# Decay attention with two MLPs: two of three parts of queries and keys loaded as 104 and 24 rows, whole tokens rebuilt by VectorE behind the attention

## The chip, the cores and the metric

One core of one Trainium2 chip runs the whole program. The metric is device time in microseconds; before the change the median of three runs is 563.14 us (562.85 to 564.15). TensorE multiplies (its weight loads are shown as PEld), VectorE is DVE, ScalarE ACT, GpSimd POOL; SyncE (SP) issues most loads, which sixteen DMA engines carry.

## The reference

The inputs are q, k, v of shape (2, 8, 768, 64) and one decay per head. Tokens are taken in 12 chunks of 64:

```python
intra = np.einsum('bhic,bhjc->bhij', qb, kb) * Dmask[None]
intra = np.einsum('bhij,bhjd->bhid', intra, vb)
inter = np.einsum('bhid,bhde->bhie', qb * lam_pow[None], kv_state)
out[:, :, sl] = intra + inter
kv_state = lam_block * kv_state + np.einsum('bhsd,bhse->bhde', kb * rev_pow[None], vb)
```

The 1536 tokens of 512 values then go through two MLPs, 512 to 2048 to 512: the first with the gate `h * clip(h + 3, 0, 6) / 6`, the second with the gate `max(0.01 h, h)`. All in float32; the weights come as 64-bit words, of which the kernel makes float32 values by shifting and joining bits.

## The kernel before

**Attention.** For each chunk c of both batches: SP loads three parts of queries and keys (`load_qk`: part 0 queries, part 1 keys for the scores, part 2 keys in natural order) and, for two chunks at once, values (`load_v`). ScalarE copies the queries into PSUM (`queries`, tile `pair`), TensorE computes scores beside them (`s`), VectorE multiplies by the decay mask into `r` (`mask`), GpSimd scales the keys into `kd` (`k_decay`, two operations), TensorE makes the state (`t`, tile `a`) and the output (`o`, tile `h`), and ScalarE copies the state into the next chunk's values (`state_copy`, two). One copy of half of the values stands in another place of the tile `vs` (`part_v`): by ScalarE for chunks 0 to 2, by VectorE for 3 to 11. The output becomes tokens as a rounded part xh (ScalarE) and the rest xl (VectorE), `att_x`. For chunks 0 to 7 ScalarE also copies the output whole into `x_spare` (`att_spare`, line 362). Each of the pieces s, t, o is 32 matmuls in the trace.

**MLPs.** Weights are prepared by half slices (l, f, j): load (`raw`), two ScalarE activations, four VectorE operations, a ScalarE rounding (wh, line 457) and a VectorE difference (wl, line 461); `w0` holds four of a first matrix, `w1` five of a second. Slices f = 0 to 3 of the first MLP are multiplied directly, tile after tile (`gemm1`, `gemm2`). From f = 4 on, two token tiles and two slices form a two by two product with seven instead of eight products (`pair`): that takes sums of weights (S1 to S4; `w_sum`, `s_high`, `s_low`, tile `s`) and differences of tokens T1 to T4 (`sums_1`: `x_diff`, line 682, on the tokens in `x_spare`; then hi and lo parts by `x_split`, line 688 the lo). The spare tokens and the sums of weights share the two buffers `s`.

**Order.** `Order` is a list scheduler in Python: every operation has an engine, a guessed time, a due time (carried back from those who use it) and buffers that it takes and frees. It starts, of what is ready, the operation with the earliest due time as soon as its engine is free, and the engines' programs are written in that order. `DUE_C` are the attention's due times, `LATENCY` the time to another engine.

**Loads and borders.** TensorE's program comes in blocks of 256 instructions. `mm` counts them and notes the matmul 8 behind each border; `load` makes every six loads, from the sixteenth on, wait for the next border's matmul. `AT_BORDER` tells the list in which attention piece each border lies; `LOAD_ORDER` is SP's order of loads.

Lines: 148 all matmuls, 154 loads, 249 and 294 kd, 287 values, 312 queries, 320 mask, 334 state copies, 349 xl, 351 xh.

Of the kernel before, what the change touches and what calls it, by code (L numbers as in the profile page):

```python
# [36 lines left out]
T_FIRST, T_STEP, T_COLLECT, HOP = 40.0, 5.45, 2.0, 0.3  # L37
LATENCY = {"dma": 2.0, "pe": 0.15, "act": 0.15, "dve": 0.15, "pool": 0.15}
N_WARM, T_WARM = 9, 4.4
# [4 lines left out]
FIRST_LOADS, LOADS_PER_BLOCK = 15, 6  # L44
AT_BORDER = (('o', 0), ('s', 2), ('t', 3), ('s', 5), ('s', 6), ('s', 8), ('o', 8), ('s', 10))
LOAD_ORDER = (('qk', 0), ('v', 0), ('qk', 1), ('qk', 2), ('v', 2), ('qk', 3), ('qk', 4), ('v', 4), ('qk', 5), ('qk', 6), ('v', 6), ('qk', 7), (0, 0, 0), ('qk', 8), ('v', 8), ('qk', 9), ('qk', 10), ('v', 10), (0, 0, 1), ('qk', 11))
# [75 lines left out]
def decay_attention_two_mlps(ctx: ExitStack, tc: tile.TileContext, qkk, vv, lam, w1, w2, out):  # L122
    nc = tc.nc
    eng = {"act": nc.scalar, "dve": nc.vector, "pool": nc.gpsimd}

    sizes = {"raw": 3, "cv": 3, "cl": 2, "w0": 4, "w1": 5, "st": 2, "s": 2, "G": 3, "u": 3, "h": 2, "a": 2, "r": 3, "vs": 3}
    late = {"Gx": 3, "ux": 3}
    const = ctx.enter_context(tc.tile_pool(name="const", bufs=1))
# [23 lines left out]

    def load(out, in_):
        i = nc.sync.dma_start(out=out, in_=in_)  # L154
        k = (len(loads) - FIRST_LOADS) // LOADS_PER_BLOCK
        loads.append(i)
        if 0 <= k < len(AT_BORDER):
            tc.add_manual_dep(i.ins, borders[min(k, len(borders) - 1)].name, mybir.DependencyInfo(
                mybir.DependencyClass.Sync, mybir.DependencyReason.DATA), reason="behind the border")

# [98 lines left out]
    op_warm = add(("pe", T_WARM / 2), lambda _: dense(N_WARM - N_WARM // 2), -800, after=[op_lam])  # L259
    op_a = add(("dve", 1.5), consts_a, -100, takes=["u"] * 3 + ["r"])  # L260
    op_steps = add(("dve", 1.25), consts_b, -100, after=[op_lam, op_a], frees=["h"])
# [5 lines left out]
    def load_qk(c):  # L267
        def fn(_):
            for i in range(3):
                load(QK[c % NQ][:, i], qkk[c, :, i])  # L270
        return fn

    def load_v(c):

        def fn(_):
            vp = new("vs", [P, 2, 2, H, D], F32)
            VS[c], VS[c + 1] = vp[:, 0], vp[:, 1]
            for i in range(2):
                load(vp[:, i, 0], vv[c + i])
            if c == 0:  # L280
                nc.gpsimd.memset(vp[other[1], 0, 1], 0.0)
        return fn
# [70 lines left out]

    SPARE = {}

    def att_spare(c):
        def fn(_):
            j, i = divmod(c, SPT)
            if not i:
                SPARE[j] = pool["s"].tile([P, 2, 2, TT], F32, tag="s", name="x_spare")  # L360
            x = SPARE[j].rearrange("p j k (c b i) -> p (j k) c b i", c=SPT, b=2)[:, :, i]
            nc.scalar.copy(out=x, in_=PA["o", c])
        return fn

    x_ready, spared = {}, {}
    ld = {}
    for c in range(NSC):
        d = due_c[c] - 2.0
        ld["qk", c] = add(("dma", 2.05), load_qk(c), d, takes=["q"])
        ld["vp", c] = ld["vp", c - 1] if c % 2 else add(("dma", 1.4), load_v(c), d if c else 0.0, after=[ld["qk", c]], takes=["vs"])  # L370
        ld["v", c] = add(("act", 0.6 if c else 1.2) if c < 3 else ("dve", 0.5), part_v(c), d - 1.0, after=[ld["vp", c]])
    pieces = {}
    st, copies, masks, dense_ops, att_ops = {}, {-1: []}, [], [op_warm], []
    for c in range(NSC):
        d, last = due_c[c], c + 1 == NSC
        ks = [] if last else [add(("pool", 1.05), k_decay(c, b), d,
                                  after=[ld["qk", c], op_scan[b], st.get(c - 2)]) for b in ((1, 0) if c else (0, 1))]
        pe = ("pe", 1.15)
        qc = add(("act", 1.2) if c else ("none", 0.0), queries(c), d - 0.5, after=[ld["qk", c]], takes=["pair"])
        s = pieces["s", c] = add(pe, scores(c), d, after=[qc, op_warm])  # L380
        m = add(("dve", 1.13), mask(c), d + 1.2, after=[s, qc, op_const], takes=["r"] if c else [], frees=["pair"])
        masks.append(m)
        if c < 2:
            op_rows[1 - c] = add(("dve", 1.4), decay_rows(1 - c), d + 4.0, after=[m])
        add(("none", 0.0), nothing, after=[s, qc] + ks, frees=["q"])
        if not last:
            st[c] = pieces["t", c] = add(pe, state(c), d + 1.3, after=ks + [ld["v", c]] + copies[c - 1] + ([op_rows[c % 2]] if c else []),
                        takes=["a"])
            copies[c] = [add(("act", 0.58), state_copy(c, b), after=[st[c], ld["v", c + 1]]) for b in range(2)]
            add(("none", 0.0), nothing, after=copies[c], frees=["a"])  # L390
        o = pieces["o", c] = add(pe, attn_out(c), d + 2.6, after=[m, ld["v", c]] + copies[c - 1], takes=["h"])
        add(("none", 0.0), nothing, after=[o, st.get(c)], frees=["vs"] * (c % 2) + ["r"])
        for n, a in (("s", s), ("t", st.get(c)), ("o", o)):
            i = N_DENSE.get((n, c), 0)
            dense_ops += [add(("pe", 0.22 * i), lambda _, i=i: dense(i), d + 5.0, after=[a])] if i else []
        hi = add(("act", 0.58), att_x(c, False), d + 4.0, after=[o])
        x_ready[c] = add(("dve", 0.69), att_x(c, True), d + 5.0, after=[hi])
        if c < 2 * SPT:
            spared[c] = add(("act", 0.58), att_spare(c), d + 5.0, after=[hi], takes=["s"] * (not c % SPT))
        add(("none", 0.0), nothing, after=[x_ready[c], spared.get(c)], frees=["h"])  # L400
        att_ops += [x_ready[c], m, o, *ks, *copies.get(c, []), *([st[c]] if c in st else [])]
# [13 lines left out]
    def load_w(h):  # L415
        def fn(_):
            l, f, j = h
            RAW[h] = new("raw", [P, DM, 2], U32)
            raw, w = RAW[h].rearrange("p n t -> p (n t)"), (w1, w2)[l][f, j].bitcast(U32)
            for a in (slice(0, DM), slice(DM, 2 * DM)) if l + f < 2 else (slice(0, 2 * DM),):  # L420
                (load if h in LOAD_ORDER else nc.sync.dma_start)(raw[:, a], w[:, a])
        return fn
# [63 lines left out]

    composed, low = {}, {}
    for l in range(2):
        for f in range(NF):
# [11 lines left out]
            if paired(l, f) and f % 2:  # L501
                p, i = f // 2, None
                for n in range(4):
                    i = add(("dve", 0.43), w_sum(l, p, n), after=[composed[l, f - 1, 0], composed[l, f, 0], i])
                hi = add(("act", 1.05), s_high(l, p), after=[i], takes=["s"])
                s_ready[l, p] = add(("dve", 1.22), s_low(l, p), after=[hi], frees=["raw"])
                add(("none", 0.0), nothing, after=[i, low[l, f - 1, 0], low[l, f, 0]], frees=["cv"] * 2)
# [144 lines left out]

    XT, CS = {}, {}
    A_B = (("A11", "B11"), ("S1", "T1"), ("S2", "T2"), ("A12", "B21"), ("S3", "T3"), ("S4", "B22"), ("A22", "T4"))
# [22 lines left out]
    def spare(k, n):  # L677
        i = {"B11": 0, "T1": 0, "B21": 1, "T4": 1, "B12": 2, "T3": 2, "B22": 3, "T2": 3}[n]
        return SPARE[i // 2][:, i % 2]

# [3 lines left out]
    def x_split(k, n, lo, src):  # L684
        def fn(_):
            xh, xl = XT[k, n]
            if lo:
                nc.vector.tensor_tensor(out=xl, in0=src(k, n), in1=xh.bitcast(F32), op=ALU.subtract)
            else:
                nc.scalar.copy(out=xh, in_=src(k, n))  # L690
        return fn

# [280 lines left out]

    def sums_1():
        u = ("dve", 1.22)
        for n, t in (("B11", 0), ("B21", 0), ("B22", 1)):
            x_op[0, 0, n] = x_of(PAIR[t])
        t1 = add(u, x_diff(0, "T1", "B12", "B11", spare), after=list(spared.values()))
        t3 = add(u, x_diff(0, "T3", "B22", "B12", spare), after=[t1])
        t2 = add(u, x_diff(0, "T2", "B22", "T1", spare), after=[t3])  # L980
        t4 = add(u, x_diff(0, "T4", "B21", "T2", spare), after=[t2])
        for n, after in (("T1", [t2]), ("T2", [t4]), ("T4", [t4]), ("T3", [t3, last1[0, PAIR[1]]])):
            splits(0, 0, n, [op_late, *after], spare)
        done = [x_op[0, 0, n][0] for n in ("T1", "T4", "T3", "T2")]
        for d in (done[:2], done[2:]):
            add(("none", 0.0), nothing, after=d, frees=["s"])
# [72 lines left out]

    sums_1()  # L1060
    for b in range(SINGLE, len(BLOCKS[0])):
# [45 lines left out]
```

## Time and profile before

| | us |
|---|---|
| median of three runs | 563.14 |
| the profiled execution's own time | 563.63 |
| its span | 561.9 |
| TensorE busy | 548.5 |
| VectorE busy | 411.9 |
| ScalarE busy | 362.3 |
| GpSimd busy | 67.5 |

The span goes from the first to the last instruction. Busy times are sums over the instructions of an engine; one that waits is not busy. In a timeline row the bracket gives how long the engine had stood idle before the row and what ended that. "issue" there is time in which the engine waited for nothing that the profile shows. TensorE's granted clock is 1.0 in every stretch.

### The profile page before, as it was taken

To read this page: it belongs to the slowest core of one execution; us is meant where nothing else is said; L and a number is where in the kernel's file an instruction comes from. 1 tells how busy PE (TensorE), PEld (TensorE's weight loads), DVE (VectorE), ACT (ScalarE), POOL (GpSimd) and SP (SyncE) were. 2 spreads that over 40 slices of the span, in tenths; PEclk is the share of its full clock that TensorE was granted. 3 is DMA by queue.
4 is the path that set the end of the run, shared out by engine and by line. 5 is a ranking of instruction groups with operands and counts; after the bars stand their busy time and mean duration, and the time that the engine had idled before them with its cause. 6 is when DMAs were issued, how large, how long until landed. Compare 5 with 4: busy or idle time off the path is not lost.

```text
span 561.9 us, 9098 instructions
## 1 busy us (share of the span) xinstructions
PE 548.5 (98%) x3512; PEld 458.2 (82%) x3512; DVE 411.9 (73%) x690; ACT 362.3 (64%) x634; POOL 67.5 (12%) x77
## 2 busy tenths in 40 slices
PE   8888999999999999999999999999999999999996
PEld 5877888888788888888888888888888888888885
DVE  7879999987987974787689897686368943782342
ACT  5988895667666745578676886687268825683220
POOL 7651001101111101101000000000110110110000
PEclk9999999999999999999999999999999999999999
DMA  8984334534447433534200402241434622512332
GB/s 312 315 296 172 113 112 94 128 116 113 86 109 190 115 84 75 130 114 93 76 1 1 157 31 80 71 150 38 94 81 124 168 56 43 132 42 50 75 73 77
DMA packets 25596, 61.66 MB, mean 110 GB/s; under 512 B 3026, under 2 KB 3282, under 8 KB 25554
## 3 DMA queue, kind: packets, MB, share of 16 engines
q1 hardware_dynamic: 18672, 48.77, 26.8%
q0 software_dynamic: 6480, 11.80, 12.3%
q8 instruction: 27, 0.44, 0.4%
q10 hardware_dynamic: 402, 0.52, 0.3%
q14 instruction: 15, 0.12, 0.1%
HBM read 46.14 MB, written 3.15 MB: 88 GB/s over the span
## 4 chain that ended last, share of the span: by engine, by line
PE 90%; DVE 4%; DMA 2%; ACT 1%; issue 1%; POOL 1%; SPq 0%; DVEq 0%; POOLq 0%; ACTq 0%
PE acc L148 44%; PE h L148 27%; PE a L148 18%; DMA sums<-st 1%; DVE r L320 1%; DMA vs<-vv 1%; PE pair L148 1%; POOL kd L294 1%; DVE vs L287 1%; DVE t L441 0%; DVE u L550 0%; DVE t L451 0%; SPq L154 0%; DVE decay L242 0%; DVE Gl L563 0%
## 5 line engine op out<-in xcount | busy, mean ns | idle before, releaser
L580 POOL DMA_DIRECT2D sums<-st x45 | 39.5, 926 | 426.0 <-ACT st L636 426.0
L148 PE MATMUL acc<-Gl,wh 128*128 128x512 f32 x136 | 53.1, 390 | 0.1
L148 PE MATMUL acc<-Gh,wh 128*128 128x512 f32 x136 | 53.1, 390 | 0.0
L148 PE MATMUL acc<-Gh,wl 128*128 128x512 f32 x136 | 53.0, 390 | 0.0
L148 PE MATMUL acc<-wl,Gh 128*128 128x512 f32 (+1 forms) x128 | 49.6, 388 | 0.0
L148 PE MATMUL acc<-wh,Gh 128*128 128x512 f32 (+1 forms) x128 | 49.6, 387 | 0.0
L148 PE MATMUL acc<-wh,Gl 128*128 128x512 f32 (+1 forms) x128 | 49.5, 387 | 0.0
L451 DVE CUSTOM_DVE_ANT_0 t<-t,c 128x1024 uint16<-128x1024 uint16 x64 | 45.0, 704 | 2.2
L636 ACT COPY st<-acc 128x512 f32<-128x512 f32 x43 | 25.1, 587 | 32.1 <-PE acc L148 15.9
L428 ACT ACTIVATE c<-raw 128x512 uint32<-128x512 uint32 x64 | 42.7, 669 | 4.7 <-DVE t L451 3.1
L449 DVE SCALAR_TENSOR_TENSOR t<-raw,t 128x512 uint32<-128x512 uint32 x64 | 44.1, 688 | 1.1
L457 ACT CAST wh<-t 128x512 fp32r<-128x512 f32 (+1 forms) x64 | 37.7, 593 | 9.1 <-DVE t L451 6.2
L432 ACT ACTIVATE t<-raw 128x512 f32<-128x512 f32 x64 | 42.6, 667 | 0.0
L461 DVE TENSOR_TENSOR wl<-t,wh 128x512 fp32r<-128x512 f32 (+1 forms) x64 | 41.2, 652 | 0.7 <-ACT wh L457 0.4
L148 PE MATMUL a<-xh,wh 128*128 128x512 f32 (+1 forms) x108 | 38.9, 360 | 0.0
L566 DVE TENSOR_TENSOR Gl<-u,Gh 128x512 fp32r<-128x512 f32 x32 | 22.1, 689 | 22.9 <-ACT Gh L754 22.7
L148 PE MATMUL h<-xh,s 128*128 128x512 f32 x112 | 38.7, 390 | 0.0
L148 PE MATMUL a<-xh,wl 128*128 128x512 f32 (+1 forms) x108 | 38.7, 358 | 0.0
L148 PE MATMUL a<-xl,wh 128*128 128x512 f32 (+1 forms) x108 | 38.7, 358 | 0.0
L638 DVE TENSOR_TENSOR sums<-acc,sums 128x512 f32<-128x512 f32 x26 | 17.9, 690 | 28.0 <-PE acc L148 28.0
L438 DVE TENSOR_SCALAR t<-t 128x512 f32<-128x512 f32 x64 | 27.0, 422 | 15.3 <-ACT t L432 15.2
L760 ACT ACTIVATE u<-a 128x512 f32<-128x512 f32 x24 | 14.3, 597 | 25.8 <-PE a L148 25.8
(176 smaller groups left out, 1447.2 us busy)
## 6 DMA issues: line engine op xcount, KB each, us to landing
raw<-w SPq DMA_DIRECT2D x58, 512.0 KB, 3.3
sums<-st POOLq DMA_DIRECT2D x45, 256.0 KB, 4.1
sums<-qkk SPq DMA_DIRECT2D x36, 256.0 KB, 4.9
vs<-vv SPq DMA_DIRECT2D x12, 256.0 KB, 5.1
raw<-w SPq DMA_DIRECT2D x12, 256.0 KB, 4.1
out<-sums SPq DMA_DIRECT2D x19, 128.0 KB, 2.3
out<-sums ACTq DMA_DIRECT2D x3, 128.0 KB, 2.7
out<-sums SPq DMA_DIRECT2D x2, 64.0 KB, 2.3
```

The lines of the kernel that those rows point to most:

```text
L148: i = nc.tensor.matmul(out, a, x, **flags)
L428: nc.scalar.activation(out=CV[h][1], in_=RAW[h][:, :, 0], func=AF.Copy, scale=2.0 ** -29)
L432: return lambda _: nc.scalar.activation(out=CV[h][0].bitcast(F32), in_=RAW[h][:, :, 1].bitcast(F32), func=AF.Abs)
L438: nc.vector.tensor_scalar(out=t.bitcast(F32), in0=t.bitcast(F32), scalar1=MAG_MIN, scalar2=MAG_MAX, op0=ALU.max, op1=ALU.min)
L449: nc.vector.scalar_tensor_tensor(out=t, in0=RAW[h][:, :, 1], scalar=0xC0000000, in1=t, op0=ALU.bitwise_and, op1=ALU.bitwise_or)
L451: nc.vector.tensor_tensor(out=t, in0=t, in1=c, op=ALU.add)
L457: nc.scalar.copy(out=W[h][0][:, cols(*h)], in_=CV[h][0].bitcast(F32)[:, cols(*h)])
L461: return lambda e: eng[e].tensor_tensor(out=W[h][1][:, cols(*h)], in0=CV[h][0].bitcast(F32)[:, cols(*h)], in1=W[h][0].bitcast(F32)[:, cols ...
L566: nc.vector.tensor_tensor(out=gl, in0=U[s], in1=gh.bitcast(F32), op=ALU.subtract)
L580: return lambda _: nc.gpsimd.dma_start(out=SUM[t][:, e, :], in_=STAGE[t, e], accum_op=ALU.add)
L636: nc.scalar.copy(out=STAGE[t, e], in_=ps)
L638: nc.vector.tensor_tensor(out=acc, in0=ps, in1=acc, op=ALU.add)
```

## The change

Loads: from chunk 3 on, parts 1 and 2 of `load_qk` are two DMAs each, rows 0 to 103 and 104 to 127, and the parts come in the order 0, 2, 1. A load of two pieces counts once for the borders, and both pieces wait. `AT_BORDER` names other pieces.

Tokens: `att_spare` goes. `sums_1` rebuilds whole tokens as hi plus lo on VectorE (`x_whole`, four operations), after `op_late`, that is after all of the attention; the four differences come behind them. The tile `s` is opened with the late buffers, and the first sum of weights waits for the last whole token.

Values: the copies for odd chunks from 3 on are ScalarE's, those for even ones stay with VectorE.

List times: the load latency, masks, kd, values, and two set-up operations get other times.

```diff
-LATENCY = {"dma": 2.0, "pe": 0.15, "act": 0.15, "dve": 0.15, "pool": 0.15}
+LATENCY = {"dma": 2.5, "pe": 0.15, "act": 0.15, "dve": 0.15, "pool": 0.15}
-AT_BORDER = (('o', 0), ('s', 2), ('t', 3), ('s', 5), ('s', 6), ('s', 8), ('o', 8), ('s', 10))
+AT_BORDER = (('o', 0), ('o', 1), ('s', 4), ('t', 4), ('o', 5), ('s', 8), ('t', 8), ('o', 9))
+FEWER = (slice(0, 104), slice(104, 128))
+FEWER_FROM, FEWER_QK, FEWER_V, FEWER_RAW = 3, (1, 2), (), ()
...
-    sizes = {"raw": 3, "cv": 3, "cl": 2, "w0": 4, "w1": 5, "st": 2, "s": 2, "G": 3, "u": 3, "h": 2, "a": 2, "r": 3, "vs": 3}
-    late = {"Gx": 3, "ux": 3}
+    sizes = {"raw": 3, "cv": 3, "cl": 2, "w0": 4, "w1": 5, "st": 2, "G": 3, "u": 3, "h": 2, "a": 2, "r": 3, "vs": 3}
+    late = {"s": 2, "Gx": 3, "ux": 3}
...
-    def load(out, in_):
-        i = nc.sync.dma_start(out=out, in_=in_)
+    def load(out, in_, fewer=False):
         k = (len(loads) - FIRST_LOADS) // LOADS_PER_BLOCK
-        loads.append(i)
-        if 0 <= k < len(AT_BORDER):
-            tc.add_manual_dep(i.ins, borders[min(k, len(borders) - 1)].name, ...
+        loads.append(k)
+        for p in FEWER if fewer else (slice(0, P),):
+            i = nc.sync.dma_start(out=out[p], in_=in_[p])
+            if 0 <= k < len(AT_BORDER):
+                tc.add_manual_dep(i.ins, borders[min(k, len(borders) - 1)].name, ...
...
-    op_a = add(("dve", 1.5), consts_a, -100, takes=["u"] * 3 + ["r"])
+    op_a = add(("dve", 2.8), consts_a, -100, takes=["u"] * 3 + ["r"])
...
-            for i in range(3):
-                load(QK[c % NQ][:, i], qkk[c, :, i])
+            for i in (0, 2, 1):
+                load(QK[c % NQ][:, i], qkk[c, :, i], c >= FEWER_FROM and i in FEWER_QK)
...
-        ld["v", c] = add(("act", 0.6 if c else 1.2) if c < 3 else ("dve", 0.5), part_v(c), d - 1.0, after=[ld["vp", c]])
+        ld["v", c] = add(("act", 0.6 if c else 1.2) if c < 3 else ("act", 0.6) if c % 2 else ("dve", 0.8), part_v(c), d - 1.0, after=[ld["vp", c]])
...
-        ks = [] if last else [add(("pool", 1.05), k_decay(c, b), d,
+        ks = [] if last else [add(("pool", 1.15), k_decay(c, b), d,
-        m = add(("dve", 1.13), mask(c), d + 1.2, ...
+        m = add(("dve", 1.22 if c else 1.4), mask(c), d + 1.2, ...
-            op_rows[1 - c] = add(("dve", 1.4), decay_rows(1 - c), d + 4.0, after=[m])
+            op_rows[1 - c] = add(("dve", 2.1), decay_rows(1 - c), d + 4.0, after=[m])
...
-        x_ready[c] = add(("dve", 0.69), att_x(c, True), d + 5.0, after=[hi])
-        if c < 2 * SPT:
-            spared[c] = add(("act", 0.58), att_spare(c), d + 5.0, after=[hi], takes=["s"] * (not c % SPT))
-        add(("none", 0.0), nothing, after=[x_ready[c], spared.get(c)], frees=["h"])
+        x_ready[c] = add(("dve", 0.69), att_x(c, True), d + 5.0, after=[hi], frees=["h"])
...
+    def x_whole(k, n):
+        def fn(_):
+            if n == "B11" or n == "B22" and not k:
+                SPARE[k, int(n == "B22")] = pool["s"].tile([P, 2 << k, 2, TT >> k], F32, tag="s", name=f"x_spare{k}")
+            x = [part([x[i].bitcast(F32) for x in X], k, n) for i in range(2)]
+            nc.vector.tensor_tensor(out=spare(k, n), in0=x[0], in1=x[1], op=ALU.add)
+        return fn
...
-        t1 = add(u, x_diff(0, "T1", "B12", "B11", spare), after=list(spared.values()))
+        for n, t in (("B11", 0), ("B12", 1), ("B22", 1), ("B21", 0)):
+            w[n] = last_whole[0] = add(u, x_whole(k, n), after=[op_late, last_whole.get(0), *x_of(ts[t])],
+                                       takes=["s"] * (n == "B11" or n == "B22" and not k))
+        t1 = add(u, x_diff(k, "T1", "B12", "B11", spare), after=[w["B11"], w["B12"]])
+        t3 = add(u, x_diff(k, "T3", "B22", "B12", spare), after=[t1, w["B22"]])
+        t2 = add(u, x_diff(k, "T2", "B22", "T1", spare), after=[t3])
+        t4 = add(u, x_diff(k, "T4", "B21", "T2", spare), after=[t2, w["B21"]])
...
-    sums_1()
+    sums_1(0)
+    od.ops[s_at[0, starts[0][SINGLE] // 2]][3].append(last_whole[0])
```

## Rows read from the trace of the kernel before

**Rows 1.** The page, part 4: the chain that ended last, share of the span.

```profile
PE 90%; DVE 4%; DMA 2%; ACT 1%; issue 1%; POOL 1%; SPq 0%; DVEq 0%; POOLq 0%; ACTq 0%
```

**Rows 2.** Stretches: us; PE, PEld, DVE, ACT, POOL busy (count); PEclk, DMA share, GB/s.

```profile
10.00:46.00 36.00, 30.18 (x871) 27.57 (x868) 29.05 (x34) 31.11 (x56) 21.84 (x20) 1.00 0.93 318
46.00:60.00 14.00, 14.00 (x230) 11.71 (x225) 13.83 (x21) 12.68 (x23) 0.00 (x0) 1.00 0.27 91
60.00:78.00 18.00, 18.00 (x81) 14.87 (x81) 17.41 (x29) 16.51 (x32) 0.00 (x0) 1.00 0.40 128
78.00:108.00 30.00, 30.00 (x134) 24.86 (x133) 27.22 (x46) 20.77 (x35) 4.54 (x5) 1.00 0.45 116
...
160.00:560.00 400.00, 396.21 (x1908) 332.43 (x1906) 271.82 (x471) 240.41 (x425) 28.84 (x33) 1.00 0.33 86
```

**Rows 3.** Timeline, TensorE in the attention: start, us, engine, what, count, idle before.

```profile
14.40 1.15 PE L148 MATMUL h<-r,vs 128*64 128x64 f32 x32 [0.87 <-DVE r L320]
...
22.21 1.15 PE L148 MATMUL h<-r,vs 128*64 128x64 f32 x32 [0.78 <-DVE r L320]
...
25.75 1.15 PE L148 MATMUL pair<-sums 64*64 64x64 f32 x32 [0.24 <-ACT pair L312]
...
29.52 1.15 PE L148 MATMUL h<-r,vs 128*64 128x64 f32 x32 [0.60 <-DVE r L320]
...
31.84 1.97 PE L148 MATMUL pair<-sums 64*64 64x64 f32 x61 [0.91 <-issue]
...
44.54 0.30 PE L148 MATMUL a<-vs,kd 128*64 128x64 f32 x2 [1.23 <-POOL kd L294]
```

**Rows 4.** Timeline of the same stretch, ScalarE and VectorE.

```profile
11.89 0.59 ACT L362 COPY x_spare<-h 128x512 f32<-128x512 f32 x1
...
12.52 0.69 DVE L349 TENSOR_TENSOR xl<-h,xh 128x512 fp32r<-128x512 f32 x1 [1.41 <-ACT x_spare L362]
...
19.62 1.28 DVE L287 COPY vs<-vs 64x512 f32<-64x512 f32 x1
...
20.93 1.22 DVE L320 TENSOR_TENSOR r<-pair,decay 128x1024 f32<-128x1024 f32 x1
...
26.36 1.84 DVE L287 COPY vs<-vs 64x512 f32<-64x512 f32 x2
...
43.22 0.62 ACT L457 CAST wh<-t 128x512 fp32r<-128x512 f32 x1 [1.11 <-DVE t L451]
```

**Rows 5.** Groups by line and form, 0 to 62 us: busy, mean ns, idle before.

```profile
L362 ACT COPY x_spare<-h 128x512 f32<-128x512 f32 x8 | 4.7, 586 | 0.0
...
L287 DVE COPY vs<-vs 64x512 f32<-64x512 f32 x9 | 7.0, 799 | 0.2
...
L682 DVE TENSOR_TENSOR x_spare<-x_spare 128x1024 f32<-128x1024 f32 x2 | 2.4, 1220 | 0.0
```

**Rows 6.** Timeline: a wait for keys, its state product, two issues by SP.

```profile
22.10 2.18 POOL L294 TENSOR_TENSOR kd<-sums,decay 64x512 f32<-64x512 f32 x2 [1.49 <-DMA sums<-qkk]
...
27.82 1.10 PE L148 MATMUL a<-vs,kd 128*64 128x64 f32 x32
...
28.12 0.86 SPq L154 DMA_DIRECT2D vs<-vv  x2
```

**Rows 7.** Behind the attention: timeline of VectorE, weights and sums of weights.

```profile
71.27 0.69 DVE L461 TENSOR_TENSOR wl<-t,wh 128x512 fp32r<-128x512 f32 x1
...
76.95 1.31 DVE L461 TENSOR_TENSOR wl<-t,wh 128x512 fp32r<-128x512 f32 x2
...
100.16 1.22 DVE L484 TENSOR_TENSOR s<-raw,s 128x1024 fp32r<-128x1024 f32 x1
```

**Rows 8.** The chain in order of time, behind the attention: start, us, what, count.

```profile
72.47 2.72 PE h L148 x12
...
77.91 2.72 PE h L148 x12
...
111.91 2.72 PE h L148 x12
```

More of the change, by code (lines that the diff above doesn't have):

```diff
@@ L151, in mm @@
         records[0] += 4 if a.dtype == F32 else 2
-    def load(out, in_):
-        i = nc.sync.dma_start(out=out, in_=in_)
+    def load(out, in_, fewer=False):
         k = (len(loads) - FIRST_LOADS) // LOADS_PER_BLOCK
-        loads.append(i)
-        if 0 <= k < len(AT_BORDER):
-            tc.add_manual_dep(i.ins, borders[min(k, len(borders) - 1)].name, mybir.DependencyInfo(
-                mybir.DependencyClass.Sync, mybir.DependencyReason.DATA), reason="behind the border")
+        loads.append(k)
+        for p in FEWER if fewer else (slice(0, P),):
+            i = nc.sync.dma_start(out=out[p], in_=in_[p])
+            if 0 <= k < len(AT_BORDER):
+                tc.add_manual_dep(i.ins, borders[min(k, len(borders) - 1)].name, mybir.DependencyInfo(
+                    mybir.DependencyClass.Sync, mybir.DependencyReason.DATA), reason="behind the border")
     starts = [[sum(bs[:i]) for i in range(len(bs) + 1)] for bs in BLOCKS]
@@ L278, in fn @@
             for i in range(2):
-                load(vp[:, i, 0], vv[c + i])
+                load(vp[:, i, 0], vv[c + i], c >= FEWER_FROM and i in FEWER_V)
             if c == 0:
@@ L352, in att_x @@
         return fn
[L354 to L365, printed above, removed]
+    x_ready = {}
     ld = {}
@@ L380, in decay_attention_two_mlps @@
         s = pieces["s", c] = add(pe, scores(c), d, after=[qc, op_warm])
-        m = add(("dve", 1.13), mask(c), d + 1.2, after=[s, qc, op_const], takes=["r"] if c else [], frees=["pair"])
+        m = add(("dve", 1.22 if c else 1.4), mask(c), d + 1.2, after=[s, qc, op_const], takes=["r"] if c else [], frees=["pair"])
         masks.append(m)
         if c < 2:
-            op_rows[1 - c] = add(("dve", 1.4), decay_rows(1 - c), d + 4.0, after=[m])
+            op_rows[1 - c] = add(("dve", 2.1), decay_rows(1 - c), d + 4.0, after=[m])
         add(("none", 0.0), nothing, after=[s, qc] + ks, frees=["q"])
@@ L419, in fn @@
             raw, w = RAW[h].rearrange("p n t -> p (n t)"), (w1, w2)[l][f, j].bitcast(U32)
-            for a in (slice(0, DM), slice(DM, 2 * DM)) if l + f < 2 else (slice(0, 2 * DM),):
-                (load if h in LOAD_ORDER else nc.sync.dma_start)(raw[:, a], w[:, a])
+            for i, a in enumerate((slice(0, DM), slice(DM, 2 * DM)) if l + f < 2 else (slice(0, 2 * DM),)):
+                if h in LOAD_ORDER:
+                    load(raw[:, a], w[:, a], i in FEWER_RAW)
+                else:
+                    nc.sync.dma_start(out=raw[:, a], in_=w[:, a])
         return fn
@@ L485, in s_low @@
                                               in1=SB[l, p][:, 0].bitcast(F32), op=ALU.subtract)
-    composed, low = {}, {}
+    composed, low, s_at = {}, {}, {}
     for l in range(2):
@@ L504, in decay_attention_two_mlps @@
                     i = add(("dve", 0.43), w_sum(l, p, n), after=[composed[l, f - 1, 0], composed[l, f, 0], i])
-                hi = add(("act", 1.05), s_high(l, p), after=[i], takes=["s"])
+                hi = s_at[l, p] = add(("act", 1.05), s_high(l, p), after=[i], takes=["s"])
                 s_ready[l, p] = add(("dve", 1.22), s_low(l, p), after=[hi], frees=["raw"])
@@ L651, in store @@
         return fn
-    XT, CS = {}, {}
+    XT, CS, SPARE = {}, {}, {}
     A_B = (("A11", "B11"), ("S1", "T1"), ("S2", "T2"), ("A12", "B21"), ("S3", "T3"), ("S4", "B22"), ("A22", "T4"))
@@ L677, in spare @@
     def spare(k, n):
-        i = {"B11": 0, "T1": 0, "B21": 1, "T4": 1, "B12": 2, "T3": 2, "B22": 3, "T2": 3}[n]
-        return SPARE[i // 2][:, i % 2]
+        i = {"B11": 0, "T1": 0, "B12": 1, "T3": 1, "B22": 2, "T2": 2, "B21": 3, "T4": 3}[n]
+        return SPARE[k, 0][:, i] if k else SPARE[k, i // 2][:, i % 2]
     def x_diff(k, n, a, b, src):
@@ L972, in splits, with sums_1 @@
         x_op[l, k, n] = [add(("dve", 0.61 * u), x_split(k, n, True, src), after=[hi])]
-    def sums_1():
-        u = ("dve", 1.22)
+    last_whole = {}
+    def sums_1(k):
+        u, ts = ("dve", 0.61 * (2 - k)), (2, 2) if k else PAIR
         for n, t in (("B11", 0), ("B21", 0), ("B22", 1)):
-            x_op[0, 0, n] = x_of(PAIR[t])
-        t1 = add(u, x_diff(0, "T1", "B12", "B11", spare), after=list(spared.values()))
[L979 to L985, printed above, removed]
+            x_op[0, k, n] = x_of(ts[t])
+        w = {}
+        for n, t in (("B11", 0), ("B12", 1), ("B22", 1), ("B21", 0)):
[5 more added lines that the diff above has]
+        t4 = add(u, x_diff(k, "T4", "B21", "T2", spare), after=[t2, w["B21"]])
+        for n, after in (("T1", [t2]), ("T2", [t4]), ("T4", [t4]), ("T3", [t3, last1[0, ts[1]]])):
+            splits(0, k, n, after, spare)
+        done = [x_op[0, k, n][0] for n in ("T1", "T3", "T2", "T4")]
+        for d in (done,) if k else (done[:2], done[2:]):
             add(("none", 0.0), nothing, after=d, frees=["s"])
```

## The prediction

> **What bounds the kernel now.** I read the chain of waits first: nine tenths of it are TensorE's own matmuls [rows 1], so a change counts only where TensorE stands still. The table by stretches says where that is [rows 2]: from 46 us on TensorE is busy without a gap up to 108 us, and from 160 to 560 us it lacks 3.8 of 400 us; between 10 and 46 us, in the attention, it is busy 30.18 of 36, so 5.82 us stand idle. In the same stretch ScalarE is busy 31.11 us, VectorE 29.05, and the DMA engines have a share of 0.93. In the stretch from 46 to 78 us the roles are other: VectorE is busy 13.83 of 14 and 17.41 of 18 us, TensorE wholly.
>
> Then I went through TensorE's starts in the attention and took each with an idle time before it [rows 3]: 0.87, 0.78, 0.60, 0.91 and 1.23 us, and twice 0.24 (one row stands for both), 4.87 of the 5.82. The releasers differ: three waits for the mask (r, VectorE), two for the copied queries (pair, ScalarE), one in which nothing but TensorE's instruction supply ("issue") is late, and one put down to kd. Each has to be paid or removed by another part of the change.
>
> **Spare copies leave the attention.** Eight ScalarE copies of 0.586 us go, 4.7 us [rows 5]. One shows its harm: the copy at 11.89 us lies ahead of VectorE's subtraction, which waits 1.41 us in all and starts at 12.52, just as the copy ends [rows 4]; the next mask stands behind the subtraction on VectorE, and TensorE behind the mask (the 0.87). Without the copy the subtraction can start when the cast ahead of the copy ends, up to 0.59 us earlier; I count 0.5 of the 0.87, as the tail of a copy lies over its neighbour's start. The two waits of 0.24 for copied queries stand behind the same queue; I count both together at 0.3, as ScalarE is given new work.
>
> **Odd values to ScalarE.** VectorE's nine copies of values take 7.0 us, 0.80 each in the mean [rows 5]. The one at 19.62 takes 1.28, and the mask starts behind it at 20.93; two at 26.36 take 1.84 together, and they stand ahead of the next mask [rows 4]. Behind these masks TensorE waits 0.78 and 0.60 [rows 3]. Taking one of each pair away moves the mask by 0.9 (half of the pair) to 1.28 us, enough for both waits: 1.4 us. The price is five copies on ScalarE (chunks 3, 5, 7, 9, 11), 0.6 us each by the spare copy's row (512 elements as well, over twice the partitions), 3.0 us against the 4.7 saved. So ScalarE comes out 1.7 us ahead over all, less where both odd values and spare copies fall, which is why I gave its own two waits no more than 0.3. These copies wait for a load in ScalarE's order; queued behind them are the state copies, the queries and the casts, for which TensorE waits. If a load is late there, its whole lateness is TensorE's; that is in the first rival.
>
> **The stretch from 39 to 46 us.** The 1.23 us before 44.54 [rows 3] come while VectorE is the late engine: the two halves of the state copy, which that product needs, run on ScalarE behind a cast at 43.22 that waited 1.11 us for VectorE's weight work [rows 4]. That work has one odd value ahead of it, 0.80 in the mean, and it goes; I count 0.9 with the last of the spare copies, between nothing (the list puts something else there) and 1.23.
>
> **Loads in two pieces.** Chunks 3 to 11 get two more DMAs each, 18 in all. An issue costs SP 0.43 us (two in 0.86, [rows 6]), so 7.7 us of SP's time; the DMA engines carry the same bytes. The trace has no load of 104 or 24 rows. From below, the pieces may give back the wait for instructions, 0.91 us [rows 3], if its fetch finds less queued before it; from above, 12 of the 18 fall on chunks 3 to 8, while the DMA engines are nearly full, and 12 x 0.43 = 5.2 us of late landing is the most that the issues alone can do. Part 2, the natural keys, moves ahead of part 1; the row at 22.10 shows GpSimd waiting 1.49 us for such a load [rows 6], and the state product of that chunk starts at 27.82, 3.5 us after the two kd operations end at 24.28. So lateness up to some 3.5 us is covered there. I take a loss of 0.4 for both and no gain for the fetch: nearer to the covered side, as 6 loads of a border period need about 9 issues, 3.9 us, and four pieces of 1.15 us take 4.6.
>
> [...]
>
> **Whole tokens behind the attention.** Four sums of hi and lo are new on VectorE, and the four differences wait for them. All have the form of the difference, 128x1024 in 1.22 us [rows 5]: 4.9 us new, and the two differences that stood before 62 us move out of the attention's end, 2.4. So VectorE gets 7.3 us more between 60 us and the first use. The cover: VectorE idles 0.59 + 2.78 us from 60 to 108 [rows 2], and the sums of weights, last of that chain, start at 100.16, end 1.22 later, and are used from 111.91 [rows 7, 8], 10.5 us of lead. 3.4 + 10.5 = 13.9 > 7.3, so TensorE sees nothing at the first pair product, even when it comes 3 us earlier. It is nearer at the weights: wl at 71.27 ends at 71.96 for matmuls from 72.47 and the third of them uses it, and of the two at 76.95 the first ends at about 77.6 for 77.91 [rows 7, 8]. The lead is some 0.3 to 0.5 us (0.8 to 1.0 with the two matmuls before). TensorE can come earlier only as far as VectorE does. Before 78 us VectorE loses two differences (2.4), two odd values (0.9 to 2.0), and the other two differences (2.4) as long as no new sum is put in their holes: 3.3 to 6.8 us, more than the gain. I cost this at nothing.
>
> **List times and border names.** These change the order only. Where the list's time was too short (0.5 for a copy that takes up to 1.28), the new one fits the rows better. I give it nothing by itself, and 0.6 us either way in the range, the size of a difference of one operation in a queue.
>
> **Sum.** 0.5 + 0.3 + 1.4 + 0.9 - 0.4 = 2.7 us. The profiled execution took 563.63 us, its span 561.9 with 1.7 around it; it becomes 560.9. It lies 0.49 above the median of the three runs, 563.14, so the median becomes 560.4. What can be told from no change is 0.2%, 1.1 us.
>
> **Rivals.**
> (1) The loads come late and eat the gain. For it: the DMA share is 0.93 over the whole stretch, and GpSimd already waits 1.49 us for a load of keys [rows 2, 6]. Against it: the cover of 3.5 us. Half of the 5.2 us late, with TensorE 2.7 earlier, exceeds a cover of 3.5 by 1.8: 0.9 of the gain is left, 562.2; with all of the gain lost 563.1. [...]
> (2) Everything goes: the seven waits and the rest of the 5.82 us but the part of the first (0.37), with the fetch. 5.4 us, 557.7. Against it: ScalarE had 31.11 of 36 us of work and keeps about 30.
> (3) Slower: new sums are taken up early. The list starts whatever is ready when VectorE is free, and behind the attention eight operations of 1.22 us are ready at once. If six stand ahead of the weights of 72 and 78 us, 7.3 us, against 4.4 freed for certain to be elsewhere (two differences and two odd values at their longest), VectorE is 2.9 late, and with 0.9 of lead TensorE stands 2.0 us at 72 to 78, and the attention's gain is not passed on: 565.1. It decides from the third sum on: with two, 2.4 us, the freed time pays.
> (4) The fetch gets worse: six borders lie between 15 and 42 us, one costs 0.91 now. If four do, 2.7 more, the gain is gone: 563.1.
>
> **Chances.** Forecast 0.52, rival (2) 0.12, (1) 0.16, (3) 0.12, (4) 0.08. Faster by over 1.1 us holds the forecast, (2) and a little of (1), and loses a little of the forecast's low side: 0.64. Within: 0.20, from (1), (4) and that side. Slower: 0.16, (3) and the worse part of (1) and (4). The likeliest case alone has 558.8 to 561.8; the range reaches to rival (2) below and to the start of (3) above, 557.6 to 564.2.
>
> **What would show it.** TensorE's busy time between 10 and 46 us, or the idle time in it, falls from 5.82 to about 3; TensorE's two waits for r behind copies of values are gone; VectorE's copies of values are five fewer; no wait of TensorE between 46 and 110 us. The share and GB/s of the DMA engines in 10 to 30 us, and GpSimd's waits for keys, decide on the pieces; the idle time with releaser "issue" decides on the fetch. I am wrong if TensorE waits for wl between 60 and 80 us, if ScalarE waits for values, or if the idle time comes back as waits for loads.

## The result: slower by 0.9%

| | before | after |
|---|---|---|
| median of 6 runs (us) | 563.57 (562.85 to 564.77) | 568.83 (567.66 to 570.28) |
| profiled execution, its span | 563.63, 561.9 | 570.28, 568.5 |
| TensorE busy in the span | 548.5 | 550.0 |

The ratio is 1.0092 (1.0073 to 1.0111). The forecast was 560.4 us, at most 564.2: the change is slower where a gain was expected, and by more than any of the rivals allowed. The page's chain that ended last answers [rows 1]; its second line has the shares by line and tile.

```profile
PE 88%; DMA 7%; ACT 1%; DVE 1%; SPq 1%; issue 1%; POOL 1%; DVEq 0%; ACTq 0%; POOLq 0%
PE acc L150 45%; PE h L150 26%; PE a L150 17%; DMA sums<-qkk 4%; DMA raw<-w 2%; DMA sums<-st 1%; SPq L159 1%; POOL kd L297 1%; PE pair L150 0%; ACT u L538 0%; DVE decay L245 0%; ACT pair L315 0%; DVE a L736 0%; DVE u L542 0%; ACT st L628 0%
```

Transfers hold 7% of the span where they held 2%, and "sums<-qkk", the loads of queries and keys, 4% by themselves. The stretches (columns as in [rows 2]; 60 to 160 replaces the last two stretches there) say where:

```profile
10.00:46.00 36.00, 27.47 (x746) 25.26 (x742) 19.23 (x23) 26.09 (x46) 18.29 (x17) 0.95 0.94 251
30.00:40.00 10.00, 6.00 (x163) 5.39 (x165) 3.00 (x4) 6.37 (x12) 3.46 (x4) 0.99 0.99 242
40.00:50.00 10.00, 8.94 (x226) 8.30 (x223) 8.14 (x11) 7.99 (x14) 6.16 (x6) 0.84 0.87 242
46.00:60.00 14.00, 11.77 (x268) 10.31 (x268) 11.67 (x17) 11.07 (x20) 3.96 (x4) 1.00 0.87 253
60.00:160.00 100.00, 99.64 (x495) 82.14 (x492) 91.61 (x150) 72.68 (x125) 7.95 (x9) 1.00 0.37 98
```

TensorE stands idle 8.53 us of the first 36 (before 5.82), and 2.23 between 46 and 60, where it had no gap [rows 2]. The DMA engines are as full as before, 0.94, and move 251 GB/s instead of 318; the loads are therefore not done at 46 us, and the share stays at 0.87 up to 60, where it was 0.27. Between 40 and 50 us the granted clock is 0.84: it is 0.50 from 39.8 to 43.0 and 1.00 from 43.2 on, behind 10 us in which TensorE had been busy for 6.00; that the one brought the other is not shown. Two pieces show the clock, 1.97 and 1.74 us where such a piece takes 1.15 [rows 3]:

```profile
28.00 0.97 PE L150 MATMUL a<-vs,kd 128*64 128x64 f32 x26 [0.91 <-issue]
...
32.51 0.30 PE L150 MATMUL a<-vs,kd 128*64 128x64 f32 x2 [1.46 <-issue]
...
38.32 0.30 PE L150 MATMUL a<-vs,kd 128*64 128x64 f32 x2 [1.77 <-issue]
...
39.90 1.97 PE L150 MATMUL h<-r,vs 128*64 128x64 f32 x31
41.80 1.74 PE L150 MATMUL pair<-sums 64*64 64x64 f32 x32
```

The account against the kernel before: 2.71 us more idle in 10 to 46, 2.23 in 46 to 60, 0.25 in 60 to 160 (0.36 against 0.11), and 1.5 of TensorE's own time, nearly all of it the two pieces at the lower clock (0.82 + 0.59), 6.7 us together; the spans differ by 6.6. The medians differ by 5.3: the profiled execution is the slowest of the six.

Who waited for loads, 10 to 60 us (total, times, longest):

```profile
POOL kd L297 <- DMA sums<-qkk: 8.7, 5, 2.9
...
ACT vs L290 <- DMA vs<-vv: 5.0, 2, 3.3
```

GpSimd's waits for keys were 3.5 us before. VectorE waited 4.4 us for values. TensorE's waits in 10 to 62 us are 10.7 in all, most of them here:

```profile
PE a L150 <- issue: 4.1, 3, 1.8
PE h L150 <- DVE u L542: 1.6, 1, 1.6
PE pair L150 <- DMA sums<-qkk: 1.2, 2, 1.0
PE pair L150 <- ACT vs L337: 1.1, 2, 0.7
PE h L150 <- issue: 0.9, 1, 0.9
PE pair L150 <- issue: 0.7, 1, 0.7
```

"issue" has 5.7 us of them (before 1.1), but it is not all instruction supply. 2.5 us fall inside a piece, as before 28.00, where the next block of 256 instructions begins: such waits, before 15.96, 21.69 and 28.00, lie 125 and 126 matmuls apart, with their weight loads 250 and 252 of the 256 (before the change 0.91, at 31.84 [rows 3]). The other 3.2, before 32.51 and 38.32, stand at the first matmuls of two state products, and these start 0.1 us after the first of ScalarE's two state copies (0.58 each) has ended. The copies stood behind work of ScalarE that had waited for loads of values and of weights:

```profile
31.19 0.61 ACT L290 COPY vs<-vs 64x512 f32<-64x512 f32 x1 [3.35 <-DMA vs<-vv]
31.83 1.18 ACT L337 COPY vs<-a 64x512 f32<-64x512 f32 x2
...
36.95 0.66 ACT L420 ACTIVATE c<-raw 128x512 uint32<-128x512 uint32 x1 [2.23 <-DMA raw<-w]
37.64 1.18 ACT L337 COPY vs<-a 64x512 f32<-64x512 f32 x2
```

With the 0.5 before the second copies, 3.7 of the 10.7 us came this way; none is put down to kd, on whose keys GpSimd waited longest.

The DMA engines' own rows show the cause (15 to 40 us; the queue of the loads: packets, MB, share of 16 engines; the first fence is of before):

```profile
DMA packets 4107, 7.57 MB, mean 303 GB/s; under 512 B 452, under 2 KB 452, under 8 KB 4101
...
q1 hardware_dynamic: 4101, 7.47, 89.5%
```

```profile
DMA packets 3436, 6.15 MB, mean 246 GB/s; under 512 B 463, under 2 KB 463, under 8 KB 3432
...
q1 hardware_dynamic: 3432, 6.08, 94.5%
```

Share x 16 x 25 us, over the packets that are not small ones under 512 B, is the mean time of one 2 KB packet: 98 ns before, 127 after (over all packets 87 and 110; the expectations below give the middle one before, 84). The bytes are the same; each row takes 30% longer.

The other rows of the list [rows 5]: the eight spare copies are gone; ScalarE's values take 0.6 us each, as costed, but waited 5.0 us for loads from 10 us on; the four sums take 1.22 each, as costed.

### The profile page after: what moved, and what is told of

The parts are those of the page before. It is cut to its first block, busy times and chain, and to the rows that moved or that the text cites. A ratio compares the mean times of both kernels' runs of the same rounds, so it can differ in the third digit from the quotient of the medians.

```text
span 568.5 us, 9119 instructions
## 1 busy us (share of the span) xinstructions
PE 550.0 (97%) x3512; PEld 459.8 (81%) x3512; DVE 412.5 (73%) x689; ACT 361.0 (63%) x631; POOL 68.0 (12%) x77
## 4 chain that ended last, share of the span: by engine, by line
PE 88%; DMA 7%; ACT 1%; DVE 1%; SPq 1%; issue 1%; POOL 1%; DVEq 0%; ACTq 0%; POOLq 0%
PE acc L150 45%; PE h L150 26%; PE a L150 17%; DMA sums<-qkk 4%; DMA raw<-w 2%; DMA sums<-st 1%; SPq L159 1%; POOL kd L297 1%; PE pair L150 0%; ACT u L538 0%; DVE decay L245 0%; ACT pair L315 0%; DVE a L736 0%; DVE u L542 0%; ACT st L628 0%
## 5 line engine op out<-in xcount | busy, mean ns | idle before, releaser
L555 DVE SCALAR_TENSOR_TENSOR Gl<-u,Gh 128x512 fp32r<-128x512 f32 x36 | 24.6, 686 | 9.3 <-ACT Gh L548 9.2
```

Source lines behind the costliest of these rows:

```text
L555: nc.vector.scalar_tensor_tensor(out=gl, in0=U[s], scalar=1.0 / 6.0, in1=gh.bitcast(F32), op0=ALU.mult, op1=ALU.subtract)
```

## The experiments

Theory R, formed from these rows: the loads' pieces make every packet slower, and all that is lost is lost there; the rest of the change gains. Rivals: the second issue by SP is the cost (I); the order of the parts or the new border names are the cost (O); the values on ScalarE are.

**e1_whole_loads.** The changed kernel with whole loads.

```diff
-FEWER_FROM, FEWER_QK, FEWER_V, FEWER_RAW = 3, (1, 2), (), ()
+FEWER_FROM, FEWER_QK, FEWER_V, FEWER_RAW = 3, (), (), ()
```

> The changed kernel with every load whole again (128 rows), all else as changed. Theory A, the pieces of 104 and 24 rows slow every packet of the loads (2 KB packets between 15 and 40 us took 84 ns in the middle before the change and 105 to 133 after it): the loss goes and the rest of the change shows its gain, 561 us (559 to 562.5), with 320 GB/s or more between 10 and 30 us. Theory B, the 18 further DMAs cost (issues, completions): the same, 561 us. Theory C, the list order, the borders, the odd values or the whole tokens cost: 567 us or more, with the idle time of TensorE in the attention still near 11 us.

561.99 us against 563.29 of before, 0.9974 (0.9958 to 0.9990). Each set against the kernel before of its own job, the pieces cost 5.26 + 1.30 = 6.6 us, and the rest of the change gains 1.3. The packet is back at 0.931 x 400 / (4348 - 487) = 96 ns:

```profile
q1 hardware_dynamic: 4348, 7.91, 93.1%
```

TensorE's idle time in 10 to 46 us falls to 3.97, and it has no gap from 46 to 160:

```profile
10.00:46.00 36.00, 32.03 (x906) 29.32 (x901) 28.16 (x32) 31.57 (x55) 22.47 (x20) 1.00 0.97 331
46.00:60.00 14.00, 14.00 (x198) 11.74 (x198) 11.60 (x21) 13.10 (x23) 0.00 (x0) 1.00 0.26 91
60.00:160.00 100.00, 100.00 (x442) 82.53 (x441) 92.13 (x151) 71.39 (x121) 10.57 (x12) 1.00 0.41 106
```

**e2_split_alone.** The kernel before with the pieces alone.

```diff
-                load(QK[c % NQ][:, i], qkk[c, :, i])
+                load(QK[c % NQ][:, i], qkk[c, :, i], c >= 3 and i in (1, 2))
```

> The kernel before with nothing but the two pieces (parts 1 and 2 from chunk 3 on, in the old order 0, 1, 2, old borders). A and B: 568 to 571 us, as the old order has less slack than the changed one. C: 563.5 us, no change.

571.93 us, 1.0148 (1.0127 to 1.0170): 8.6 us lost by the pieces alone, with the old order of parts and the old borders. So neither the order (O) nor the values are the cause; what else is in the change even took some of the loss back. A packet took 0.938 x 400 / (3501 - 472) = 124 ns.

```profile
q1 hardware_dynamic: 3501, 6.21, 93.8%
```

**e3_halves_of_columns.** As many DMAs as in the changed kernel, cut by columns: 128 rows of 1 KB.

```diff
-FEWER = (slice(0, 104), slice(104, 128))
+FEWER = (slice(0, 4), slice(4, 8))
-            i = nc.sync.dma_start(out=out[p], in_=in_[p])
+            i = nc.sync.dma_start(out=out[:, p], in_=in_[:, p])
```

> The changed kernel with the same loads in two pieces, but cut by columns: 128 rows of 1 KB each, twice. As many DMAs as the changed kernel. A: the rows lie as in a whole load, so about 561.5 us, as with whole loads. B: as slow as the changed kernel, 568 us.

563.51 us, 1.0005 (0.9992 to 1.0018); 1.5 us above e1 of the same job. That is the most that the second DMA (I) can have cost, 1.5 of the 6.6, for these pieces also have twice the packets, of 1 KB; cutting by rows is the other 5.1. The stretch from 10 to 46 us keeps its rate:

```profile
10.00:46.00 36.00, 31.86 (x903) 29.16 (x899) 26.46 (x31) 31.28 (x55) 22.55 (x20) 1.00 0.96 309
```

**e4_loads_alone.** A program of loads alone, in phases of twelve loads of 256 KB (or of a part of their rows), each phase cut in another way.

```diff
+    rows = [whole, (slice(0, 104), slice(104, 128)), (slice(0, 64), slice(64, 128)), (slice(0, 112), slice(112, 128)),
+            (slice(0, 104),), (slice(0, 24),), None, whole]
```

> Only loads, nothing of the computation: twelve loads of 256 KB (or a part) after one another in eight phases: whole; 104 and 24 rows; 64 and 64; 112 and 16; 104 alone; 24 alone; two halves of columns; whole again. A: whole loads near 340 to 400 GB/s with packets of 84 ns; 104 and 24 rows at 240 to 270 GB/s with packets of 105 to 135 ns; halves of columns above 320. 64 and 64 rows slower still if it is a matter of which rows move together. B: halves of columns as slow as 104 and 24 rows, and packets of 104 and 24 rows still 84 ns.

Stretches inside the phases (clock, DMA share, GB/s at the end): whole, 104 and 24 rows, 64 and 64, halves of columns, whole; then SP's issues in the phase of 64 and 64.

```profile
1.00:11.50 10.50, 0.00 (x0) 0.00 (x0) 1.00 0.87 300
13.00:27.50 14.50, 0.00 (x0) 0.00 (x0) 1.00 0.74 217
28.50:45.80 17.30, 0.00 (x0) 0.00 (x0) 1.00 0.65 182
...
83.00:96.00 13.00, 0.00 (x0) 0.00 (x0) 1.00 0.82 242
98.00:108.00 10.00, 0.00 (x0) 0.00 (x0) 1.00 0.90 315
```

```profile
28.38 15.26 SPq L135 DMA_DIRECT2D x<-qkk  x24
```

The loss is there without any computation beside it: 217 GB/s in 104 and 24 rows (219 in 112 and 16) against 300 to 315. By the division above a packet took 95 ns whole and 111 in 104 and 24 rows, and the engines' share fell from 0.87 to 0.74: each is about half of the loss. The phase of 64 and 64 rows tells nothing of the DMA engines, though it is the slowest: SP needed 15.3 us for its 24 issues, 0.64 each where halves of columns took 0.47, and they fill the stretch. Halves of columns, expected above 320, came to 242; their 24 issues take 11.3 of some 13 us, so that phase, too, is in good part SP's. (e4, e11, e13 and e14 are one execution each.)

**e1_again, e5_five_in_flight, e7_values_back, e8_spares_back.** With the pieces out, what is the rest worth? e1 was run again as the base; e5 lets each load wait for the fifth before it; e7 gives all values from chunk 3 on back to VectorE; e8 puts the spare copies back into the attention and takes the whole tokens away. e7 and e8 name the borders by the pieces that fit their order.

```diff
+            flights.append(i.ins)
+            if flying >= IN_FLIGHT:
+                tc.add_manual_dep(i.ins, flights[flying - IN_FLIGHT].name, ...
```

```diff
-... if c < 3 else ("act", 0.6) if c % 2 else ("dve", 0.8), part_v(c), ...
+... if c < 3 else ("dve", 0.8), part_v(c), ...
```

```diff
+            spared[c] = add(("act", 0.58), att_spare(c), d + 5.0, after=[hi], takes=["s"] * (not c % SPT))
-            w[n] = last_whole[0] = add(u, x_whole(k, n), ...
```

> The changed kernel with whole loads once more, as the base of the three below: 561.3 to 562.3 us, and again 2.5 us or more of TensorE's idle time between 10 and 46 us with the releaser 'issue'.

> The changed kernel with whole loads, where each load of the attention also waits until the fifth load before it has landed (up to eight were under way before). Theory F, what is left idle is TensorE's instruction fetch queued behind loads: the waits put down to 'issue' between 10 and 46 us fall from some 3 us to under 1.5, and the time to 560.5 us. Rival G, the fetch is late for another reason (the border's own distance): the waits stay, 562 us, or more where loads become late.

> The changed kernel with whole loads, and all values from chunk 3 on copied by VectorE again (0.8 in the list), borders named anew. By the prediction's terms, 1.4 us for the odd values and half of the 0.9 in the stretch from 39 to 46 us come back: 563.5 us, with waits of 0.5 us and more for r. Rival: the odd values are worth nothing, since ScalarE pays as much: 562 us.

> The changed kernel with whole loads, but the spare copies by ScalarE in the attention and the differences in its holes, as before the change; borders named anew. By the prediction's terms 0.5 + 0.3 us come back, and half of the 0.9: 563.1 us. Rival: the whole tokens behind the attention cost as much on VectorE as they save: 562 us or less.

In one job, with before at 563.38: e1_again 562.22 (ratio 0.9985, 0.9972 to 0.9997), e5 563.43 (1.0012, 1.0000 to 1.0024), e7 564.44 (1.0027, 1.0011 to 1.0043), e8 562.77 (0.9992, 0.9981 to 1.0002). So the values on ScalarE are worth 2.2 us, and the exchange of spare copies for whole tokens 0.55, which the two intervals do not tell from nothing. TensorE's waits in 10 to 62 us, one fence each for e1 (the first run), e5 and e8:

```profile
PE a L150 <- issue: 1.4, 2, 1.2
PE pair L150 <- issue: 1.0, 2, 0.9
PE h L150 <- issue: 0.8, 2, 0.4
PE pair L150 <- ACT pair L315: 0.3, 1, 0.3
```

```profile
PE a L151 <- POOL kd L303: 2.2, 2, 1.1
PE pair L151 <- DMA sums<-qkk: 1.1, 1, 1.1
...
PE pair L151 <- issue: 0.2, 1, 0.2
```

```profile
PE pair L150 <- ACT pair L315: 3.9, 5, 1.0
PE h L150 <- DVE r L323: 0.9, 1, 0.9
```

With the spare copies in the attention (e8) TensorE waits 3.9 us for queries and 0.9 for a mask and never for its instructions; without them (e1) 0.3 for queries, none for masks, and 3.2 by "issue", 3.0 of it where a block begins. So waits for instructions stand in the place of two thirds of those that went. With five loads under way (e5) "issue" falls to 0.2, but kd and the keys come 3.3 us late instead, and the time, expected at 560.5, is 1.2 above that of e1_again. Whether the instructions now found less queued before them, or the late keys hid them as the queries do in e8, this run cannot tell.

e7's price was expected as waits for masks. They did not come back: its waits in 10 to 62 us are by "issue" (4.0, with 1.60 of it at 47.80) and for other ScalarE work, and TensorE has 1.33 us of gaps in 60 to 160. So the size of that term stands and its path, in this execution (1.6 us above e7's median), was another one.

**e9_six_in_flight, e10_old_part_order, e12_six_old_order.** e1 with six loads under way; e1 with the parts in their old order; both.

```diff
-            for i in (0, 2, 1):
+            for i in range(3):
```

> The changed kernel with whole loads and each load waiting for the sixth before it. With five the waits for instructions fell from 3.2 to 0.2 us but 3.9 us of waits for kd and keys came in their place. If a middle exists: issue waits under 1.5, waits for loads under 1.5, 561 us. If the two only trade: 562.2 to 563.4 us.

> The changed kernel with whole loads and the three parts in the old order 0, 1, 2. The prediction set the new order at nothing next to a cover of 3.5 us: 562.2 us, within 0.5 of whole loads in the new order. Rival: kd is now late for the state product and 1 us is lost: 563.2 us. Rival: the new order makes the scores late, and the old one gains 0.5 to 1 us.

> Whole loads, six in flight and the old part order together, on the changed kernel's list. Each alone gave 0.9977 of the time before. If each takes away other waits (six in flight those for instructions, the old order those for keys): 560.8 us, a ratio of 0.996. If both only move the same waits about: 561.8 us, 0.9975.

e9 561.90 (0.9977, 0.9962 to 0.9992), e10 561.58 (0.9977, 0.9963 to 0.9991), with before at 563.26; e12 in a later job 562.46 (0.9968, 0.9947 to 0.9988), before 563.46. The order of the parts makes no difference that these runs can tell. Six under way win nothing, and their waits by "issue" are not settled: 1.4 us in e9, under half of e1's, but 4.5 in e12, the most of all runs with whole loads:

```profile
PE a L151 <- issue: 2.5, 2, 2.1
PE h L151 <- issue: 1.5, 2, 0.9
```

Whether e12 is any faster than the others is inconclusive. With whole loads e1, e9, e10 and e12 are faster than the kernel before by 0.15 to 0.3%.

**e11_which_rows.** Why rows? Twelve loads a phase of one set of rows each; Q is one more rival to R.

```diff
+    rows = [(slice(0, 128),), (lo,), (hi,), (even,), (odd,), (slice(0, 32),), (slice(0, 128, 4),), (slice(24, 128),), (slice(0, 96),),
+            (slice(0, 128),)]
```

> Only loads: phases of twelve loads each, of 128 rows; rows 0 to 63; 64 to 127; every second row from 0; every second from 1; 0 to 31; every fourth; 24 to 127; 0 to 95; 128 again. [...] Rival Q, only an uneven number of rows on each engine costs: 64, 32 and 96 rows as whole loads, 104 rows slow.

The queue's rows inside three phases: all rows, rows 0 to 63, every second row (windows of 9.5, 9.8 and 9.5 us).

```profile
q1 hardware_dynamic: 1715, 3.12, 93.4%
...
q1 hardware_dynamic: 960, 1.57, 57.6%
...
q1 hardware_dynamic: 960, 1.57, 54.7%
```

By the same division, 93, 118 and 108 ns a row, and 104 for rows 24 to 127. Each of these sets of fewer rows is slower, and 64 rows, by Q to be as fast as all rows, took 118 and 108: Q missed. But with 64 rows the engines were idle for over 40% of the time (shares of 0.58 and 0.55): the twelve loads took 10.1 and 9.5 us, of which twelve of e4's issues of 64 rows, 0.64 us each, would fill 7.7. So two more runs were made, with longer rows.

**e13_one_port_each.** Eight loads a phase, 6 KB a row.

```diff
+    rows = [slice(0, 128), slice(0, 64), slice(0, 128, 2), slice(0, 16), slice(0, 61, 4), slice(0, 121, 8),
+            slice(0, 8), slice(0, 29, 4), slice(0, 57, 8), slice(0, 128)]
```

> Only loads run; attention and MLPs are left out. Ten phases of eight loads, rows of 6 KB: all 128 rows; 0-63; every second (64); 0-15; every fourth of 0-60; every eighth of 0-120; 0-7; every fourth of 0-28; every eighth of 0-56; all 128 again. Read is the mean time of a 6 KB packet, against the whole loads (some 280 ns, three times the 92 of a 2 KB packet).
> [...]
> [...]
> [...]
> Theory E: with fewer engines at a time a packet gets faster: 8 rows in any pattern at or below the whole loads, which speaks for a limit on the sum of all engines.

Mean per 6 KB packet: whole 241 ns, rows 0 to 63 466, every second 277, rows 0 to 15 724, rows 0 to 7 710, spread sets of 8 or 16 rows 336 to 370. Rows 0 to 7 are twice as slow as eight spread ones, and none of these sets is faster than the whole loads, so E falls: which rows move counts, not their number alone. Eight rows of 0 to 28 (370) were no faster than eight of 0 to 56 (336), but the DMA share was 0.28 and 0.25 there: the engines may have had too little to do.

**e14_ports_kept_busy.** Four runs of 6 KB to a row, so that each engine always has a next packet.

```diff
+    rows = [slice(0, 128), slice(0, 64), slice(0, 128, 2), slice(0, 104), slice(104, 128), slice(0, 16), slice(0, 61, 4),
+            slice(0, 8), slice(0, 57, 8), slice(0, 29, 4), slice(0, 128)]
+            src = qkk[c * R:(c + 1) * R].rearrange("r p i h c -> p r (i h c)")
```

> Only loads run; attention and MLPs are left out. Three loads a phase, each with four runs of 6 KB to a row, so that an engine always has more to do. [...] Phases now: all rows; 0-63; every second; 0-103; 104-127; 0-15; every fourth of 0-60; 0-7; every eighth of 0-56; every fourth of 0-28; all rows.
> [...]
> [...]

By the same division, a 6 KB packet took 237 ns in whole loads, 235 in every second row and 482 in rows 0 to 63; 478 in rows 0 to 103 and 484 in rows 104 to 127; of 16 rows, 925 in rows 0 to 15 and 497 in every fourth of 0 to 60; of 8 rows, 924 in rows 0 to 7, 498 in every eighth of 0 to 56 and 275 in every fourth of 0 to 28. So sets of one size differ by 1.9 to 3.4 times. Stretches for all rows, rows 0 to 63, every second, 0 to 103, 104 to 127:

```profile
4.00:25.00 21.00, 0.00 (x0) 0.00 (x0) 1.00 1.01 420
30.00:51.00 21.00, 0.00 (x0) 0.00 (x0) 1.00 1.00 205
56.00:66.00 10.00, 0.00 (x0) 0.00 (x0) 1.00 1.02 425
71.00:114.00 43.00, 0.00 (x0) 0.00 (x0) 1.00 0.82 168
119.00:128.00 9.00, 0.00 (x0) 0.00 (x0) 1.00 0.75 152
```

Rows 0 to 63 keep all engines busy and move half. The changed kernel's two pieces keep 0.82 x 16 = 13 and 0.75 x 16 = 12 engines busy and move 168 and 152 GB/s. So two things slow such a piece: packets that take twice as long, 478 and 484 ns against 237, and engines that get nothing. That the first is also what lengthened the 2 KB packets inside the kernel (30%, where long rows show 100%) fits, but was not shown by itself. Each phase read and wrote the same set of rows, so no run shows which end is the slow one. Open is also why every second row keeps 425 GB/s and rows 0 to 103 do not: the trace names neither the engine of a packet nor where it writes.

## Why the prediction was wrong

**The step that failed** is "Loads in two pieces": a loss of 0.4 was taken, and the runs show 6.6 (e1) to 8.6 (e2). The bounds were wrong, not only the value between them. "From above" counted SP's 12 issues of 0.43 us and said that the DMA engines carry the same bytes; but they were at 0.93 [rows 2], so what counts is their time per byte, for which the trace of before had no row, and which had to be bounded too. In the 25 us from 15 on, (303 - 246) x 25 us = 1.4 MB fewer were moved, 4.7 us of loads at 303 GB/s: near the size of the loss. The issues, the only cost that was bounded, are part of 1.5 (e3).

In e14 the two pieces keep 13 and 12 of the 16 engines busy, and idle engines are about half of what the pieces lose in e4 (shares of 0.87 and 0.74). Inside the kernel the engines' share did not fall, 94.5% against 89.5%: there it is the longer packet that counts, and that stood in no term and no rival.

**Rival (1)**, late loads, is what happened, with the wrong end: it was allowed to eat the gain and no more, because half of 5.2 us stood against a cover of 3.5. The cover itself held: GpSimd waited 8.7 us for keys, and none of TensorE's waits is put down to kd. The largest part was lost at ScalarE, which waited 5.0 us for values and 3.7 for weights with the state copies queued behind (3.7 of TensorE's 10.7 us). The prediction said that such lateness would be wholly TensorE's and named it as its refutation, but gave it no price.

**Spare copies and whole tokens** (0.8 and 0): 0.55 measured (e8), not clear of noise. The cover of the whole tokens was right: no gap of TensorE from 46 to 160 us in e1, and the weights' lead held. **Rival (3)**, sums taken early, did not occur: with whole loads TensorE has no wait at 72 to 78 us.

**Odd values** (1.4): 2.2 (e7), by another path than the masks.

**The stretch from 39 to 46 us** (0.9): not gained. In e1 1.16 us of "issue", at the beginning of a block, stand there before 45.71, in place of the 1.23 [rows 3]:

```profile
45.71 0.34 PE L150 MATMUL a<-vs,kd 128*64 128x64 f32 x4 [1.16 <-issue]
```

**The fetch** (0, and rival (4) at 2.7): 3.0 us at the beginnings of blocks in e1 against 0.91, 2.1 worse. The terms without the loads came to 3.1 us, and 3.1 - 2.1 = 1.0 is near the 1.2 to 1.3 that e1 and e1_again gained. Rival (4) was right with whole loads, and its chance of 0.08 was too low. **List times and order**: nothing (e10), as costed.

## What to carry to other kernels

Where DMA engines are full, an edit that keeps the bytes but changes the shape of a load has to be priced in time per packet, and a shape that no row shows is unbounded until one is measured: a kernel of loads alone gives it in one run. If a load must be cut, cut it by columns and keep all 128 rows (e3: 563.5 us, the rows' pieces 568.8). And when waits are removed from an engine one after the other, look at what supplies its instructions: with whole loads it took back some 2 of the 3 us that the other terms were to gain.

## What the runs showed of the hardware

A load of fewer than 128 rows can be slow although all engines are busy: 205 GB/s for rows 0 to 63 against 420, and 425 for the same number of rows taken every second one (e14). The time of a 6 KB packet goes with which rows move: 482 ns against 235 for these two sets of 64, 924 for rows 0 to 7 against 498 for every eighth of 0 to 56 and 275 for every fourth of 0 to 28. What the slow sets have in common is not shown. Whether two transfers of 64 rows each gain over one was not measured either, as SP's issues set the pace of e4's 64 and 64 rows.

SP took longer to issue a load of 64 rows, 0.64 us from one to the next, than half of the columns of 128 rows, 0.47 (e4). Twelve loads of every second row landed in 9.5 us, of rows 0 to 63 in 10.1 (e11).

Instructions come by DMA, too, in packets of 16 KB (queue q8 of the pages): 27 of them before and after the change; TensorE's 3512 matmuls and 3512 weight loads come to 260 for each. In the changed kernel the waits at the beginning of a block, before 15.96, 21.69 and 28.00, end 1.4 to 1.6 us after such a packet has landed, at 14.59, 20.08 and 26.37; before the change the one before 31.84 ends 1.5 us after the landing at 30.36. That more loads under way delay them is not shown: by "issue" TensorE waited 0.2 us with five, 1.4 and 4.5 with six (e9, e12), and without a limit 3.2 (e1) and nothing (e8). In e1 the waits by "issue", 3.2 us, were the largest of TensorE in 10 to 62 us once the others were gone.
